# 22 filler matmuls at the head of TensorE's list, and the lists of the first two units arranged anew

## The chip, the core and the metric

The kernel runs on one core of a Trainium2 chip. Five engines work from lists of their own: TensorE (PE: matmuls and transposes; its weight loads are shown apart as PEld), VectorE (DVE), ScalarE (ACT), GpSimd (POOL) and SyncE (SP, which here only issues transfers). They wait for one another by semaphores. Transfers between HBM and SBUF run on 16 DMA engines that serve several queues: q1 is fed by SP, q0 by GpSimd, q10 by ScalarE. TensorE writes into eight PSUM banks, from which VectorE and ScalarE read. The metric is the device time of one execution, in microseconds, as a median over runs.

## The reference

For 4 batches, 8 heads, 768 positions and a head size of 64, each query keeps the 6 chunks (of 32 keys) with the highest bound, attends causally to them, and the result goes through a two-layer MLP.

```python
k_min = np.min(k_chunks, axis=3)
k_max = np.max(k_chunks, axis=3)
ub = np.sum(np.maximum(q * k_min, q * k_max), axis=-1)      # per query and chunk, shapes cut
top_chunks = np.argsort(np.where(causal, ub, -1e9), axis=-1)[..., -6:]
scores = np.where(sel & causal_in_positions, (q @ k.T) / 8, -1e9)
x = softmax(scores) @ v                                      # -> [3072, 512]
h = x @ w_in                                                 # [3072, 2048]
g = np.where(h > 0, h, np.exp(np.minimum(h, 0)) - 1)
out = g @ w_out                                              # [3072, 512]
```

## The kernel before

The 3072 rows are done in eight units of 384. Units 0 and 1 hold the first and second 192 positions of batches 0 and 1 together (in the names `p` and `s`, after the batch); units 2 to 7 are the halves of one batch each, from the second half of batch 0 on. In unit 0 no chunk has to be chosen, since at most 6 exist. For each unit the kernel loads q, k and v, transposes q and k on TensorE, takes each chunk's minimum and maximum of k on VectorE, computes the bounds, chooses, scores, takes the exponential on ScalarE, multiplies with v, divides, transposes, and runs the MLP.

**An order written out by hand.** The code first records a graph of operations with `g.op`, each with the engines that it may run on. Then it walks through a string, `ORDER`: every three characters are an engine's letter (P, A, D, G, S for TensorE, ScalarE, VectorE, GpSimd, SP) and the number of an operation. A second string, `PLACES`, gives each new buffer its slot. So the strings fix on which engine an operation runs, each engine's list, and which buffer follows which in a slot. An engine works strictly along its list: an operation that waits holds up all behind it. What reads or reuses a buffer waits for the operations before it on that buffer.

**The names used below.**

- `ldk`, `ldq`, `ldv` (L304): the loads of k, q and v, into tiles `f`. Eleven such tiles exist, and a load waits until the tile's earlier readers are done. Of units 0 and 1, `ldk1s00` is k of batch 1, unit 1, its first 96 positions.
- `kT`, `qT` (L402, four matmuls each): fp32 transposes of k and q with `ident_f`. One for each batch, unit and group of four heads. `kmax`, `kmin`, `ks` (L367, L370) are the chunks' extremes; `kt`, `qh`, `qt` (L320 on ScalarE, L322 on VectorE) copy the transposes out of PSUM; `ka` copies k into the tile `lhs`.
- `tr` (L684): one 512-column bf16 matmul that puts the mask into a bank ahead of unit 0's scores `sc` (L692). It needs `identb`, a bf16 copy of the identity that GpSimd makes in `ident` (L254), and `tn0`, `tn1` (L268). `ex` (L700) is the exponential.
- `v` (L333 on GpSimd, L322 elsewhere): the cast of loaded v. `pv` (L754): the product with v. `rcp`, `on` (L636, L646 on VectorE, L643 on ScalarE): the division. `px` and `xt` (L669): transposes of the result and their copies.
- `w_in0`, `w_in1`, `w_in2` (L291): loads of w_in, issued by GpSimd, columns for the groups fc 0 to 3, 4 to 7 and 8 to 15. `w_out0` to `w_out3` (L297) likewise.
- `h0.fc` (L851, four matmuls): the MLP's first layer for unit 0; `e`, `m`, `g` (L858, L860, L864) its activation; `o0.t.c` (L875) the second layer. `h0.4` to `h0.7` need w_in1, `h0.0` to `h0.3` w_in0, the others w_in2.
- `ub` (L592): the bound matmuls; `ubT`, `max`, `lt`, `sT` on VectorE (L603 to L620) choose the chunks; `mk` copies the choice into the tile that the scores of unit 1 (L728) read.
- Constants: `zeros`, `rz`, `sz`, `pz`, `pu`, `kz`, `ez`, `vz`, `kq` (memsets, L247), `es` (L276), `oh`, the one-hot pattern (L282, L285, 25 memsets), `tris` (L263), `ec` (L304, a transfer of the constant `econst` into `lhs`).

**Fillers.** The graph also holds 170 operations `fill`, each one matmul on the bf16 tile `zeros`. The string of before names none of them, so none runs:

```python
fills.append(g.op("fill", (PE,), lambda e, bank=bank: nc.tensor.matmul(
    ap(bank)[:, 0:256], lhsT=zeros[:, 0:P], rhs=zeros, start=True, stop=True),
    reads=[(fixed, "zeros")], writes=[(bank, 0)], after=fills[-2:-1]))
```

The walk through the strings:

```python
for j in range(0, len(order), 3):
    o = g.ops[64 * DIGITS.index(order[j + 1]) + DIGITS.index(order[j + 2])]
    for b in o.bufs:
        if b.slot is None and b.cls != "fixed":
            b.slot = DIGITS.index(next(places))
    o.emit({"P": PE, "A": ACT, "D": DVE, "G": POOL, "S": SP}[order[j]])
```

Of the kernel before, what the change touches and what calls it, by code (L numbers as in the profile page):

```python
# [39 lines left out]
G0iS0WD01A02D09D06S0sG0kD0jG0aS0yD03D00D0qG0mG0bA0VG04D05G0eS0uG0cG0dA0tS0rS0vS0xD0lD0oS0wS0YS0X  # L40
P0MD0OD0QS0BP1oP0DP1aP11S0ZS0zD0ED0NA0HA0IG0fG0gD0FP0KP1pA1eG0pP1kA0LD1bP0TA0RA15A17G16P1jP1tP1l
S0+D0UP1qP1uD1cP18A1nD13S2gS2fG0CA1rP1hD19A1sG0nP1zD12S2hS2iP1yA1iP1AA1gA1mGmED0PA1CP1vA1xA1BG0A
P1DP26P25P1ED10G0-S2PS2vS2OD27D28D1FA1wP1YP20P2aGmDA0SP29D2bP1XA2cP1+D21G0JP1IP1OP1RP1SP1HS2IP2o
P1ND1GD1JD1ZD1KP2dG1dGmFA1-P1LD2qD1PA1QD2jD22P23D1TD1UD2eA2sD24A1MS2QP1VD1WG08G2uG0hP2BD2DD2CA2t
Pm-Pn6G2EAn7GbsGmGPn2Gn8D2pG2rAm+Dn0D14D0GAn3Dn4P2wPmWA2xA2yS2RP2JA2KDn5D2zPmSPmODn9Dn1AmXAmTD2L
GmYPnaGmHDmZAmPP3lAnbGmIA2FDmQDmUPmKAmLDmVD3nD3mA2MD3pGncPnGG2HPniA2AG07GmMA1fPnCG2SAnjD3oPnuD3q
D3rPnmDmRDmNG3tPneAnHA3sGnkDndAnvGnIP3HDnlAnDPnqGnwA3IDnJP41PnyDnxAnrA3uGnEDnFP3JP3+AnfPnQDnsS2k
A3KDntD2NAnnS3fG3LP2XA42P38PnRS2mA40GmJAnzA2GDnoD2ZDnpD2YP4lGngPnKPnXA4mD3vDnhA2+A30D43D3cP4DA4E
P4FG3ePnYA4GGnAD3aA3dD39D2-D31P4jD4HP3gG3bP33PnSS32S4+A34D35PnLA3hA4kD3iG3kS2TDnBP3wD4nS2VG2lG36
D3xG3jS50PnZPn-A2nD3yD3zA37S4-D3APnMPnTD3BD3CS4YD3GA3EG3FP3NDnUP4OP4MS4XS4ZP3MD3DP48P45A4PA4NP44  # L50
G2UG2WP4aD3ODn+D3PP4IP4JA4bP3SPnNA49D46D47A3TD4cS7UP3QD4QAnOP4sP4uP4dA3RP4eP4oS7SA4tP4pD4fP5rG3U
D4gA4vP4RD4KD4LP4SP4hA5sP5QS7WD4TD4UP3VP3WA5RD4qP5fP4VD3XD3YA5gS7RP5ED4rG4wP4xA4WP4yD5SP3ZA5FD4z
P58D4AA5iS57P5kD5aA4iP4BA4CG7VS53P5JD3-P5xD59G5TG5uA5cS55D5BA5oA5NPolPoJD5mA5GD5KPo5S5wAoKD5zS8l
PoxD5yGoLAo6SaND5LA5IPo9A5tDoMSo0G5bPodGo7AomD5lS51AoyG5MPohDo8G5nAoaSnPGonPoRA5OScZGobDooAoePoF
D7TA5hGofAoSPopDocG5AA5jGozDogPo1AoGGoTSnVDoAAoqPoBGoHDoUS7NAoiGorA5DPotDoIS7OAo2GojDosP5VAouGo3
DokA5HGovDo4A5UG5PDowA5vPoNAoCG5dD5XPp1A52G7XD5WAoOD5ZGoDPp2A5qGoPA5eD5YPpePpfD5-SnWPp7D5+SaHPp8
DoEA60G61DoQPpgD63A56DaOP66P6gA67P64DaQP6cP6iA65Pp3D62A6dDaPA6jP6mP68A6hP6lD5pP6aDaRP6eA6nPp9A69
D54SaSG6oA6fP6BP6xD6kPoVA6bS7MA6CP6vA6yS7YP6qA6wP6HS7PP6pAoWP6zA6IS7QPoZD6rGoXD6sA6AG5CP6JDoYAo-
P6tScRP6MGbmP6ND6uA6KP7bGo+P7cP76A6OP6-Dp0PphA77D6LA7dD6PShFScXG7eDaTP6FA6+Pp4ApiA6GP6DA6EP72P70
P78P6RDp5A71A79DaUP6QDaVA73P7CP74A75P6YA6ZP7xP7zA7yA7ADaWP7ZD7aD6SSb3P6WA6XPpaApbP7DSpjSp6G7BP8g  # L60
A8hD7-D81D6TD7+P7rP7lP7fP7gP7tP89P7pD8iA7EG7FD7hD7iD8aD8bG8kG8jP7vP8yD8zA7mA7sA7qA7uP7nA7oA7wP8m
P6UP8FP7GScSSaCDb4A8CD8DG8EA6VA8dG8fP7HD7ID7JA8qP7jA7kP84A85P8tA8uAaIA8vD8oP7KD7LPpkPpEPpQPpsPpM
# [36 lines left out]
DwlDwdGwgDwhPvWPwyGwsAvXDvQDvRGvYDvZPwGAwHPv-Av+DwtPw2GwIDwJAw3Dw4Dw5AwzDwAGw0Dw1PwKPwmPwQAwnGwo
DwpPwCAwDDwBPwRPwLPwSGwEDwFPwTAwUPwWPwXSwVPwMPwNDwOSwPPwYPwZAw-Sw+Px0Px1Px2Px3Dx4Sx5  # L100
"""
PLACES = """
012034567000812349a10562170103125110304017213233236458001721210034522131062120134456670324031011
2206007710050120112732140001224010263151400156000721281724932a00b64251ac1657102d30416e1437016309
# [876 lines left out]
```

## Time and profile before

| | us |
|---|---|
| median of 3 runs (280.84 to 281.32) | 281.3 |
| profiled execution | 281.25 |
| its span, first to last instruction | 279.5 |
| TensorE busy | 263.2 |
| VectorE busy | 217.4 |
| ScalarE busy | 217.1 |
| GpSimd busy | 125.5 |
| moved by the DMA engines | 38.47 MB |

How to read the rows of the profile. A row of a timeline has the start (us from the first instruction), the duration, the engine, the line of the code, the operation, what it writes and reads, the shapes, how many instructions are merged, and in brackets the idle time before with what ended it. A row of the chain of waits has the start, the length and what the chain went through: it is followed back from the last instruction, at each step to what released it. A row by window has its bounds and length, then busy time and number of instructions of TensorE, its weight loads, VectorE, ScalarE and GpSimd, and then TensorE's granted clock, the mean busy share of the DMA engines (it can pass 1 where packets overlap) and GB/s. A row of a queue has the packets, the MB and their share of the DMA engines' time. A row of a transfer's issue has the median time from issue to landing as its last number.

### The profile page before, as it was taken

The numbers are of one execution on the slowest core, as the hardware profiler recorded it, in microseconds if no ns is written. First come the engines' busy times: TensorE is split into PE (matmuls) and PEld (weight loads), VectorE is DVE, ScalarE is ACT, GpSimd is POOL, SyncE is SP. The second block draws the span as 40 slices with busy tenths as digits, with TensorE's granted clock in tenths as the row PEclk, the third lists the DMA queues.
The fourth block names the chain that finished last, engine by engine and source line by source line (L and its number), as shares of the span: only waits on it lengthen the run. The fifth ranks groups of instructions, "written<-read, shape, count | busy, mean of one in ns | idle before, by whom it ended". The sixth has DMA issues, their size and how long they took to land.

```text
span 279.5 us, 6918 instructions
## 1 busy us (share of the span) xinstructions
PE 263.2 (94%) x2436; PEld 162.9 (58%) x2436; DVE 217.4 (78%) x656; ACT 217.1 (78%) x493; POOL 125.5 (45%) x249
## 2 busy tenths in 40 slices
PE   1978899999999999999999999999999999999994
PEld 0745465785456755576555555666655556665553
DVE  4668978799978999979998999569797698424931
ACT  2596796789699998999999859886968579982620
POOL 8674745348521755422685736222541346310410
PEclk9999999999999999999999999999999999999999
DMA  8999999999529999946985499416600210042002
GB/s 163 198 211 211 199 211 210 217 202 251 123 60 203 247 219 230 196 115 112 171 203 114 109 226 206 84 36 136 170 4 0 60 39 1 16 139 82 15 17 96
DMA packets 103779, 38.47 MB, mean 138 GB/s; under 512 B 95168, under 2 KB 99520, under 8 KB 103744
## 3 DMA queue, kind: packets, MB, share of 16 engines
q1 hardware_dynamic: 98864, 33.53, 57.3%
q0 software_dynamic: 3696, 4.19, 8.7%
q10 hardware_dynamic: 1184, 0.30, 0.5%
q8 instruction: 19, 0.31, 0.5%
q14 instruction: 16, 0.13, 0.1%
HBM read 30.41 MB, written 6.29 MB: 131 GB/s over the span
## 4 chain that ended last, share of the span: by engine, by line
PE 70%; DVE 13%; DMA 8%; ACT 4%; issue 1%; POOL 1%; SPq 0%; DVEq 0%; ACTq 0%
PE bank L875 24%; PE bank L851 22%; PE bank L782 9%; DMA w_in_sb<-in_moe_w_in_dram 5%; PE bank L833 5%; DVE gT L864 2%; PE bank L592 2%; PE bank L402 2%; DMA kc<-in_k_dram 2%; ACT e L858 2%; DMA f<-in_k_dram 1%; PE bank L543 1%; PE bank L728 1%; PE bank L893 1%; DVE on L646 1%
## 5 line engine op out<-in xcount | busy, mean ns | idle before, releaser
L851 PE MATMUL bank<-xt,w_in_sb 128*128 128x384 bf16 x512 | 89.2, 326 | 2.2 <-DMA w_in_sb<-in_moe_w_in_dram 2.2
L875 PE MATMUL bank<-w_out_sb,gT 128*128 128x512 bf16 x368 | 89.5, 379 | 0.0
L860 POOL TENSOR_SCALAR m<-e 128x384 f32<-128x384 f32 x96 | 50.7, 536 | 59.3 <-ACT e L858 47.0
L864 DVE SCALAR_TENSOR_TENSOR gT<-bank,m 128x384 bf16<-128x384 f32 x128 | 65.9, 549 | 9.7 <-POOL m L860 8.4
L858 ACT ACTIVATE e<-bank 128x384 f32<-128x384 f32 x128 | 58.6, 493 | 16.7 <-PE bank L851 13.9
L851 PEld LDWEIGHTS <-w_in_sb 128*128 128x128 bf16 x512 | 49.1, 98 | 36.6 <-DMA w_in_sb<-in_moe_w_in_dram 3.0
L797 ACT ACTIVATE pt<-bank 128x384 bf16<-128x384 f32 (+1 forms) x144 | 67.0, 547 | 3.5 <-PE bank L782 2.1
L875 PEld LDWEIGHTS <-gT 128*128 128x128 bf16 x368 | 34.6, 97 | 35.7 <-issue 2.2
L782 PE MATMUL bank<-rhs,lhs 96*128 96x384 bf16 (+2 forms) x240 | 42.8, 293 | 1.0 <-DVE on L646 0.5
L814 POOL TENSOR_TENSOR pt<-pt,tri 128x256 bf16<-128x256 bf16 (+1 forms) x18 | 16.6, 924 | 39.3 <-ACT pt L801 20.1
L782 PEld LDWEIGHTS <-lhs 96*128 96x128 bf16 x240 | 21.7, 97 | 13.9 <-issue 0.9
L833 PEld LDWEIGHTS <-pt 128*128 128x128 bf16 x576 | 21.0, 97 | 4.0 <-DVE pt L814 0.4
L833 PE MATMUL bank<-vext,pt 128*128 128x65 bf16 x576 | 22.2, 193 | 0.3 <-DVE pt L814 0.3
L646 DVE TENSOR_TENSOR on<-bank,rcp 128x384 bf16<-128x384 f32 (+1 forms) x37 | 18.8, 509 | 1.2
L367 DVE TENSOR_REDUCE kst<-bank 128x12 f32<-128x384 f32 x32 | 16.6, 548 | 3.7 <-PE bank L402 2.8
L322 POOL CAST rhs<-qt 64x384 bf16<-64x384 f32 x23 | 12.3, 542 | 13.1 <-ACT qt L320 12.1
L636 DVE RECIPROCAL rcp<-bank 128x6 f32<-128x6 f32 (+1 forms) x40 | 7.3, 185 | 14.0 <-PE bank L833 8.7
L320 ACT ACTIVATE o<-bank 128x512 f32<-128x512 f32 (+1 forms) x13 | 7.5, 587 | 13.0 <-PE bank L875 10.1
L322 DVE COPY o<-bank 128x512 f32<-128x512 f32 (+1 forms) x12 | 7.9, 663 | 12.0 <-PE bank L875 10.0
L860 DVE TENSOR_SCALAR m<-e 128x384 f32<-128x384 f32 x32 | 13.1, 417 | 2.8 <-ACT e L858 2.6
L402 PE MATMUL bank<-ident_f,f 96*128 96x96 f32 x64 | 9.3, 295 | 6.2 <-DMA f<-in_k_dram 6.2
L814 DVE TENSOR_TENSOR pt<-pt,tri 128x512 bf16<-128x512 bf16 (+1 forms) x30 | 10.8, 376 | 5.3 <-ACT pt L801 3.5
(102 smaller groups left out, 338.6 us busy)
## 6 DMA issues: line engine op xcount, KB each, us to landing
f<-in_v_dram SPq DMA_DIRECT2D x22, 256.0 KB, 4.8
out_dram<-o SPq DMA_DIRECT2D x21, 256.0 KB, 3.4
f<-in_q_dram SPq DMA_DIRECT2D x18, 256.0 KB, 4.9
f<-in_k_dram SPq DMA_DIRECT2D x18, 256.0 KB, 4.7
kc<-in_k_dram SPq DMA_DIRECT2D x8, 384.0 KB, 4.3
w_out_sb<-in_moe_w_out_dram POOLq DMA_DIRECT2D x4, 512.0 KB, 10.5
f<-in_q_dram SPq DMA_DIRECT2D x6, 192.0 KB, 5.0
w_in_sb<-in_moe_w_in_dram POOLq DMA_DIRECT2D x2, 512.0 KB, 8.8
```

Of the source, the lines that this page charges most:

```text
L322: eng[e].tensor_copy(out=dst, in_=src)
L367: g.op(("kmin", "kmax")[w] + tag, (DVE,), lambda e, w=w, op=op: nc.vector.tensor_reduce(out=cs(w), in_=src(), axis=AX.X, op=op), reads=[(b ...
L646: nc.vector.tensor_tensor(out=ap(on)[:, 0:nt].rearrange("p q h d -> p h q d"), in0=view()[:, :, :, 0:D], in1=ap(rcp)[:, :, 0:nt].to_broadc ...
L782: nc.tensor.matmul(ap(banks[hd])[:, o + pc:o + pc + wd], lhsT=apl(ls, G)[0:96, pr, hd, P * kb:P * (kb + 1)], rhs=ap(rs)[0:96, hd, c0 - HS ...
L797: lambda e, hd=hd, pt=pt, banks=banks, wtot=wtot: nc.scalar.activation(out=ap(pt)[:, hd, PAD:PAD + wtot], in_=ap(banks[hd])[:, 0:wtot], fu ...
L814: eng[e].tensor_tensor(out=view, in0=view, in1=tri[:, 64:64 + P].rearrange("p (a b w) -> p a b w", a=1, b=1) .to_broadcast([P, 2, len(dg), ...
L833: nc.tensor.matmul(view()[:, hd, qi, :], lhsT=ap(pt)[:, hd, P * qi + off:P * qi + off + P], rhs=ap(vx[b])[:, kb, 2 * r + hd, :], start=(kb ...
L851: nc.tensor.matmul(ap(bank)[:, 0:HS], lhsT=w_in_sb[:, kk, P * fc:P * (fc + 1)], rhs=ap(xT[i, kk]), start=(kk == 0), stop=(kk == NKK - 1))
L858: g.op(f"e{i}.{fc}", (ACT,), lambda e, eb=eb, bank=bank: nc.scalar.activation(out=ap(eb), in_=ap(bank)[:, 0:HS], func=AF.Exp), reads=[(ban ...
L860: g.op(f"m{i}.{fc}", (POOL, DVE), lambda e, eb=eb, mb=mb: eng[e].tensor_scalar(out=ap(mb), in0=ap(eb), scalar1=-1.0, scalar2=1.0, op0=AOT. ...
L864: nc.vector.scalar_tensor_tensor(out=ap(gt), in0=ap(bank)[:, 0:HS], scalar=0.0, in1=ap(mb), op0=AOT.max, op1=AOT.min),
L875: nc.tensor.matmul(ap(bank), lhsT=ap(gts[fc])[:, P * tt:P * (tt + 1)], rhs=w_out_sb[:, fc, :], start=(fc == 0), stop=(fc == NFC - 1))
```

## The change

Three things change; no computation does.

In the graph, all fillers share one bank:

```diff
     fills = []
+    bank = Buf("bank")
     for i in range(FILL):
-        bank = Buf("bank")
         fills.append(g.op("fill", (PE,), lambda e, bank=bank: nc.tensor.matmul(
```

`ORDER` and `PLACES` are new strings. `ORDER` names 1970 operations in place of 1948: the same ones, and 22 fillers. Their last 1313 operations are the same in both, on the same engines; the slots that the strings give differ all through. The first lines of the diff:

```diff
-G0iS0WD01A02D09D06S0sG0kD0jG0aS0yD03D00D0qG0mG0bA0VG04D05G0eS0uG0cG0dA0tS0rS0vS0xD0lD0oS0wS0YS0X
-P0MD0OD0QS0BP1oP0DP1aP11S0ZS0zD0ED0NA0HA0IG0fG0gD0FP0KP1pA1eG0pP1kA0LD1bP0TA0RA15A17G16P1jP1tP1l
...
+G0iS0WD00D01PjZA02D09Pj-S0sPj+D06G0cG0aG0mG0kD0lD0qPk0Pk1G0bS0yPk2Pk3D03D0jG04D0eG0fD05G0oG0nG08
+G0gS0uPk4A0VPk5A0tS0rPk6Pk7Pk8Pk9PkaP1kPkbPkcP1oPkdPkePkfP0MPkgP11P1aA15A1ePkhPkiP1tS0xA0QG0RG0d
...
```

Spelled out by the names of the operations, the heads of the lists:

```
TensorE before: kT0p1 tr kT0p0 kT1p1 kT1p0 qT0p0 tr tr qT0p1 tr tr sc0p0 sc0p1 tr qT1p0 qT1p1 tr tr sc1p1 sc1p0
                pv (15) kT0s0 pv pxp3 pxp0 pxp2 pxp1 kT0s1 h0.4 h0.6 h0.5
                qT0s0 h0.3 qT0s1 h0.2 h0.1 h0.7 ub00 h0.0 h0.15 h0.9 ...
TensorE after:  fill x14 tr fill x2 tr fill x3 kT0p1 fill kT1p0 kT1p1 fill x2 tr kT0p0 qT0p0 qT0p1 tr tr sc0p0 tr
                qT1p1 sc0p1 qT1p0 tr sc1p1 tr sc1p0 pv (of batch 0: 8, then of batch 1: 8) pxp3 kT0s0 pxp0 pxp2
                pxp1 kT0s1 h0.4 h0.6 h0.5 qT0s0 qT0s1 h0.3 h0.1 h0.2 ub00 h0.7 h0.0 h0.9 h0.15 ...
GpSimd before:  kz vo tn0 pu tn1 ident ez1 ez0 es0 es1 oh vz0 ka01p0 v0p1 rz w_in1 v0p0 v1p0 w_in0 ka10p0 ks1p1
                w_in2 tris2 ka10s0 kq ks0s1 ky202 w_out0 m0.6 ks0s0 m0.3 w_out1 w_out2 ...
GpSimd after:   kz ez0 tn0 pu vo tn1 ident es1 sz rz tris2 oh ka00p1 es0 v0p1 w_in1 ka11p0 v0p0 ka01p0 v1p0 w_in0
                w_in2 ka11p1 ks1p1 ka10p0 vc0 ks1p0 ky202 ka10s0 kq w_out0 m0.6 qa00s0 w_out1 m0.3 w_out2 ...
ScalarE before: table ldk1p00 ldk0p10 kt0p0 ka00p0 kt1p1 qh0p0 ka00p1 kt1p0 ka11p0 ex ex ex qh1p1 ka11p1 ex x5 ka10p1
ScalarE after:  table ldk1p00 ldk0p10 kt1p0 kt1p1 kt0p1 kt0p0 qh0p0 ka00p0 ex ex qh1p1 ex x4 ka10p1 ex ex
VectorE before: warm tnz triz kp idz zeros vz1 identb pz sz kmax0p1 kt0p1 kmin0p0 kmin0p1 kmax0p0 kmin1p1 qh0p1 ...
VectorE after:  zeros warm tnz triz pz vz1 idz kp ez1 identb vz0 kmax0p1 kmin1p1 kmax1p1 kmin0p1 kmin0p0 kmax0p0 qh0p1 ...
SP before:      ldk1p10 ldk0p01 ldq0p11 ldk0p11 ldk0p00 ldq0p00 ldq0p10 ldq0p01 ldq1p10 ldq1p00 ldv0p1 ldv1p0 ldv0p0
                ldv1p1 ldk0s10 ldk0s00 ldq0s00 ldq0s10 ldk1s10 ec000 ldk1s00 ec001 ldq1s00 ldq1s10 ldv0s0 ...
SP after:       ldk1p10 ldk0p01 ldq0p11 ldk0p11 ldk0p00 ldq0p10 ldq0p00 ldq0p01 ldq1p00 ldq1p10 ldv0p1 ldv0p0 ldv1p1
                ldv1p0 ldk0s10 ldk0s00 ldq0s10 ldq0s00 ldk1s00 ec000 ldk1s10 ec001 ldq1s10 ldq1s00 ldv0s0 ...
```

29 operations of the first two units change their engine: `ez1` and `vz0` go from GpSimd to VectorE, `sz` the other way, and some copies (`ka`, `qa`, `mk`, `xt`), differences `ks`, three divisions `on` and the activation step `m0.13` move too.

More of the change, by code (lines that the diff above doesn't have):

```diff
@@ L45 @@
[L45 to L50, printed above, removed]
@@ new lines @@
+P1ED1FD0PP1YP1NP1OP1XP2aP29GmDS2IGmFG1gG1dA1wP1+P1IP1SP20G0JD2bD2cD21P1HD1ZA1GP1RG2jP2dS2RS2QG14
+D22D1JD1KD1TD1PP2oD2qA1-A2eP1LD1QD1UGbsA2sG2uP23P1VD1WA24A1MP2BD2CD2DG0hGmGPm-Am+Dn0Dn1D2EPn6An7
+Gn8Pn2An3P2wA2tA2xG2zP2JA2KA2yPmWPmOPmSDn4D2pDn5AmXGmHGmYD2rAmPA2FAmTD2LD0GP3lDmQDn9A2APnaAnbGmI
+DmZDmUPmKGncD3nD3mD3pD3oDmVG2HG07PniPnGA2MAmLGmMD3qD3rAnHA1fS2kS32DmND2SDmRA3sAnjPnuAnvPnCPneDnd
+S3fGnIDnJP3HA3IAnDA3tGnkDnlPnmPnqAnrGnwDnxS2mGnEG3uDnFDnsDntP3JPnyP3+P41AnfGngPnQD2NP2XDnhG2GA3K
+G3LA3vAnzAnnDnoPnRGmJP4lA40A42A4mD2YP4FPnKP4DA2+A4GA30D2ZDnAA4EG4HPnXP38P4jPnYDnpD3aD3cD2-A4kA3d
@@ new lines @@
+P3gP33A34D3eD39D31D3bD43S2VS2TA3hA35G3kPnLPnSD3iP3wDnBD4nPnZPnMPn-PnTD3xD3yS50S4+A3jA2nS4-G37G36
+G2lP3ND3zD3AD3BD3CG2UD3GP4MP3MA3ES4ZS4YDnUG2WG3FD3DS4XP4JA4NP4OA4PD3OD3PP44P48A49Dn+P4aP45D46A4b
+D4cP4IP3SA3TPnND47D4QP3QP4uP4sP4dP4eD4fA3RAnOG3UP4oP4pP4SP4RP5rD4gP4hA4vA4tG4wD4qD4TD4KD4LA5sP5Q
+A5RD4UP3WP3VD3XD3YD5SP5fA5gP4VA4WD4rP5EA5iA5FP4xP4yS7US7SS7RP3ZP5kP58A4iD4zD4AP4BP5JD3-D5mD5aA5c
+A4CG7VS55S5wSaNS57D59P5xD5lA5oG5TPoJA5GD5KPo5AoKD5zPoxPolD5yGoLG5uAo6D5LA5IPo9G5bGo7A5tDoMPodG5M
+AomA5NSo0S7WD5BAoyPohDo8S8lG5nAoaGonPoRA5OSnPS51S53GobDooAoePoFScZD7TA5hGofAoSPopDocG5AA5jGozDog
@@ new lines @@
+Po1AoGGoTDoAAoqPoBGoHSnVDoUAoiGorA5DPotS7NDoIAo2GojDosP5VS7OAouGo3DokA5HGovDo4A5UG5PDowA5vPoNAoC
+G5dD5XPp1A52G7XD5WAoOD5ZGoDPp2A5qGoPA5eD5YPpePpfD5-Pp7D5+SnWPp8DoESaHA60G61DoQPpgD63A56DaOP66P6g
+A67P64DaQP6cP6iA65Pp3A6dD62A6jDaPP6mP68A6hP6lP6aD5pP6eA6nDaRPp9A69G6oA6fP6BD54P6xSaSPoVA6bD6kA6C
+S7MP6vA6yP6qA6wS7YP6HP6pAoWS7PP6zA6IPoZD6rGoXD6sA6AS7QG5CP6JDoYAo-P6tP6MGbmP6ND6uA6KP7bGo+ScRP7c
+P76A6OP6-Dp0PphA77D6LA7dD6PP6FDaTPp4A6+G7eApiShFScXA6GP6DA6EP72P70P78P6RDp5A71A79DaUP6QDaVA73P7C
+P74A75P6YA6ZP7xP7zA7yA7ADaWP7ZD7aD6SSb3P6WA6XPpaApbP7DSpjSp6G7BP8gA8hD7-D81D6TD7+P7rP7lP7fP7gP7t
@@ L101 @@
+DjTPjBPvuPvEDjwDjxSjyAjIGjPAjAAjGAjEPjUAjCPjVDjWDjXSjYPvFPvvPvGPvHDvIDvwPw6Aw7SvxPvKAvLGvMDvNSvJ
+PwiPwuAwjAwvDwkPwqAwrDwwDw8Dw9PvSAvTGvUDwxPwaAwbDwcPweAwfPvOAvPDvVDwlDwdGwgDwhPvWPwyGwsAvXDvQDvR
+GvYDvZPwGAwHPv-Av+DwtPw2GwIDwJAw3Dw4Dw5AwzDwAGw0Dw1PwKPwmPwQAwnGwoDwpPwCAwDDwBPwRPwLPwSGwEDwFPwT
+AwUPwWPwXSwVPwMPwNDwOSwPPwYPwZAw-Sw+Px0Px1Px2Px3Dx4Sx5
 """
 PLACES = """
[L103 to L104 removed]
@@ L118 @@
+52600432124970010200f210001732143257083412564315422141355143620000216211622301202011040011311522
+6101022d341097031425201c00212a74612b010121326504203ef1702g61130412674052057360715647011101253570
+60132003270141475230155647203011120023200182510041210101b7226002dg1133500241c1122272601e102f6030
+1541729112071
 """
```

115 lines of the change are left out of this document (49 added, 66 removed).

## The prediction

> **What bounds the kernel now.** I read the page first, for the engine that is full and the stretch where it is not, then busy time by stretch, then the chain of waits up to 80 us, then the timelines of TensorE and GpSimd, and last the transfers.
>
> ```profile
> PE 263.2 (94%) x2436; PEld 162.9 (58%) x2436; DVE 217.4 (78%) x656; ACT 217.1 (78%) x493; POOL 125.5 (45%) x249
> PE   1978899999999999999999999999999999999994
> DMA  8999999999529999946985499416600210042002
> 0.00:6.00 6.00, 0.39 (x1) 0.18 (x1) 2.85 (x11) 1.49 (x2) 5.15 (x16) 1.00 0.83 155
> 6.00:13.00 7.00, 6.44 (x40) 4.90 (x42) 4.34 (x9) 3.09 (x7) 4.05 (x28) 1.00 1.35 203
> 21.50:31.50 10.00, 7.93 (x80) 4.74 (x80) 8.66 (x29) 6.86 (x17) 6.48 (x13) 1.00 1.17 206
> 31.80:80.00 48.20, 48.20 (x449) 30.00 (x450) 42.75 (x138) 39.05 (x86) 24.23 (x48) 1.00 0.95 189
> ```
>
> In the window rows the first pair after the length is TensorE. From 31.8 to 80 us it has no gap (48.20 of 48.20), so what reaches it earlier there reaches the end earlier, until another engine or a transfer runs out of lead. Before that it has gaps: 5.61 us of the first 6, and 2.07 of the 10 us up to 31.5. The transfer engines are full in the same stretch: their digit is 9 from the second slice on, 200 GB/s.
>
> ```profile
> 2.36 4.15 DMA f<-in_k_dram
> 17.33 0.50 POOL lhs L322
> 17.91 0.16 POOL kst L370
> 18.06 13.64 DMA w_in_sb<-in_moe_w_in_dram
> 31.75 4.07 PE bank L851 x24
> 25.89 0.82 PE L851 MATMUL bank<-xt,w_in_sb 128*128 128x384 bf16 x4 [1.04 <-DMA w_in_sb<-in_moe_w_in_dram]
> 31.75 4.07 PE L851 MATMUL bank<-xt,w_in_sb 128*128 128x384 bf16 x24 [1.19 <-DMA w_in_sb<-in_moe_w_in_dram]
> ```
>
> Five rows of the chain, two of TensorE's timeline. The chain goes from the third w_in load, issued by GpSimd at 18.06 and landed at 31.70, straight to TensorE's first matmul on it at 31.75. GpSimd issued it late: two small operations of its list stood before it. So the end is set by when w_in2 lands, not by how fast TensorE does its first 30 us.
>
> **The 22 fillers.** Each is a 256-column matmul on zeros. The rate is that of the early bf16 matmuls on the mask constant:
>
> ```profile
> 7.73 2.56 PE bank L402 x16
> 10.29 0.85 PE bank L684 x2
> 44.12 0.66 PE bank L402 x8
> 44.78 1.73 PE bank L875 x8
> 2.15 0.17 DVE L247 MEMSET zeros<- 128x128 uint32 x1
> 6.56 0.74 PE L402 MATMUL bank<-ident_f,f 96*128 96x96 f32 x3 [0.76 <-DMA f<-in_k_dram]
> ```
>
> Early, 512 columns take 0.85/2 = 0.425 us; late, 1.73/8 = 0.216. Transposes: 0.160 against 0.082. TensorE runs at half rate at first, though the granted-clock column says 1.00 throughout. A filler at the early rate costs 0.21 us. `zeros`, now first on VectorE, is ready near 1.1 us. Fourteen fillers end at 1.1 + 14 x 0.21 = 4.1. A mask matmul then needs ident_b, whose cast moves to about 4.0 to 4.5 with one more memset ahead of ident on GpSimd (an estimate); it, two fillers, a second mask matmul and three fillers bring TensorE to 4.5 + 2 x 0.425 + 5 x 0.21 = 6.4. The first key transposes can't finish before their second load, at 6.51. Nineteen fillers cost nothing under that wait; if identity or zeros came 0.5 us later they would push the transposes by 0.4. The three behind cost 0.3 to 0.6 us of TensorE's list, with 2 to 3 us of lead behind them, as follows.
>
> **What faster early matmuls are worth.** Between 6.56 and 12.63 TensorE does 6.07 us of work at half rate. If the fillers end that state by 6.5, up to 3.0 us are saved. Taken to the end, that would give 281.25 - 3.0 = 278.2. I value it at zero, since the next users are held elsewhere: unit 0's attention waits for v, which GpSimd casts, and MLP 0 for w_in. [...]
>
> **The arranged lists: GpSimd issues w_in earlier.** This is the term that I count.
>
> ```profile
> 5.99 3.10 POOL L285 MEMSET onehot<- 32x1 bf16 x24
> 11.66 0.50 POOL L322 COPY lhs<-kt 64x384 bf16<-64x384 bf16 x1 [1.98 <-ACT kt L320]
> 12.13 0.61 POOL L333 TENSOR_SCALAR vext<-f 64x512 bf16<-64x512 f32 x1
> 12.80 1.37 POOL L247 MEMSET rhs<- 32x1536 bf16 x1
> 14.12 0.98 POOL L291 DMA_DIRECT2D w_in_sb<-in_moe_w_in_dram  x1
> 15.18 1.35 POOL L333 TENSOR_SCALAR vext<-f 128x512 bf16<-128x512 f32 x2
> 16.48 0.80 POOL L291 DMA_DIRECT2D w_in_sb<-in_moe_w_in_dram  x1
> 4.48 1.12 POOL L276 TENSOR_SCALAR_AFFINE_SELECT econst<-econst 32x384 bf16<-32x384 bf16 x2
> f<-in_v_dram SPq DMA_DIRECT2D x1, 128.0 KB, 4.6
> f<-in_v_dram SPq DMA_DIRECT2D x1, 128.0 KB, 5.2
> ```
>
> Now: one-hot done at 9.1, 2 us idle for a key copy of ScalarE, v, the 1.37 us memset `rz`, w_in1 at 14.12. After: `rz` (1.37), `sz` (about 0.3) and `tris2` (about 0.25) stand ahead of the one-hot, `ez1` (half of 0.85) goes to VectorE and `es0` (0.56) behind it: 9.1 + 1.37 + 0.3 + 0.25 - 0.43 - 0.56 = 10.0. The key copy now waits for an earlier one on ScalarE and takes 0.5, es0 0.56: 11.1. Then v, whose load lands at 6.75 + 4.6 = 11.4 as before: cast to 12.1, and w_in1 issues at 12.1, 2.0 us earlier. After it 0.98, two key copies (0.5 each) and a cast (0.65) make 14.7; the next cast waits for the load issued at 9.42 that lands at 14.6: 15.4. w_in0 issues at 15.4 (1.0 earlier), w_in2, next to it, at 16.3 (1.8 earlier).
>
> What that brings at landing has two ends. The stream of three loads starts 2.0 us earlier and the transfers are full, so at best w_in2 lands 2.0 earlier, at 29.7. If the pause between w_in1 and w_in0 stays tied to w_in0's issue, it is 1.0, at 30.7. I take 1.5, between them, since w_in2's own issue moves by 1.8 but has to queue behind w_in0. TensorE's other work must be done by then. w_in1 lands about 2 us earlier, at 20.4 or so; from there eight groups h0.x (4 matmuls, 4.07/6 = 0.68 us each), 0.7 of query transposes and 0.8 of bound matmuls make 6.9, so 27.3. From w_in0's landing (25.89 less 1.0, so 24.9) five groups and the bounds make 4.2, so 29.1. It is done either way.
>
> **What is given back.** The transfers were full already, so an earlier w_in pushes the q and k loads on SP's queue.
>
> ```profile
> q0 software_dynamic: 1163, 1.68, 92.5%
> q1 hardware_dynamic: 1158, 0.35, 23.6%
> q0 software_dynamic: 471, 0.48, 96.3%
> q1 hardware_dynamic: 395, 0.10, 23.0%
> f<-in_q_dram SPq DMA_DIRECT2D x1, 192.0 KB, 23.4
> f<-in_q_dram SPq DMA_DIRECT2D x1, 192.0 KB, 5.1
> 43.95 0.82 PE L402 MATMUL bank<-ident_f,f 96*128 96x96 f32 x8
> ```
>
> The first pair is 22 to 32 us, the second 17 to 20: packets go one for one, and since those of q0 are larger, q1 falls to 0.035 MB/us. [...] In rows: the last q load of batch 1 for unit 1 is issued at 18.63 and lands 23.4 later, at 42.0; its transposes run at 43.95, so 1.95 us of lead. A gain of 1.5 uses most of it. I take off 0.1 for the places where lead runs out.
>
> Sum: 281.25 (profiled execution, span 279.5 and 1.75 around it; the median of the three is 281.3) - 1.5 + 0.1 = 279.85, that is 279.9.
>
> **The rivals.**
>
> *The early half rate was the bound*: 278.2, as worked out. For it: TensorE is full from 6 to 13. Against: the 1.04 and 1.19 us waits for w_in. Chance 0.06.
>
> *The gain is eaten by the transfers.* By 42 us as many bytes have to be moved as before. If w_out3, the next load of GpSimd, also comes 1.5 to 2 us earlier, it gets between: 512 packets beside q1's last loads, at 116 packets/us 4.4 us for both, of which half is q1's own. The q load then lands near 42.0 + 2 = 44.0, and its transposes stand where they stood, at 43.95. TensorE waits there instead of at 31.75: 281.2. Against: w_out3 hangs on GpSimd's order behind several MLP operations, and a pause of q0 just before it lets q1 catch up. Chance 0.20.
>
> *The first q loads of unit 1 starve*, the slower side. Now the second is issued at 13.24, lands at 18.3 and is through before w_in's packets come (from about 16.9, 2.8 us behind the issue). After, w_in's packets come from 14.9, when about 2 us x 0.2 MB/us = 0.42 MB of q1, 1,700 packets, is still to go ahead of it. Some 400 pass beside w_in1 in 3 us. If q0 makes no pause before w_in0, the other 1,300 go at 116 per us: 11.2 us, so it lands at 14.9 + 3.1 + 11.2 = 29.2. TensorE stands at these transposes, with 0.7 + 3 x 0.65 + 0.8 + 2 x 0.65 = 4.7 us to do before w_in2's groups: 29.2 + 4.7 = 33.9 against 31.75, 2.2 slower, 283.4. With a pause such as that of now at 20 us,
>
> ```profile
> q0 software_dynamic: 21, 0.02, 14.1%
> q1 hardware_dynamic: 1072, 0.33, 94.3%
> q0 software_dynamic: 71, 0.06, 25.0%
> ```
>
> it lands before 24 and costs nothing: the first row is 16 to 17 us, w_in's first packets, the others are 20 to 21.5, where q1 moved 0.33 MB. It decides from a landing at 31.75 - 4.7 = 27.0 on. Half a pause gives the case's middle: 282.3. Chance 0.24.
>
> **How the numbers follow.** Forecast 0.50 at 279.9, its own range 279.1 to 280.6; early clock 0.06; eaten 0.20; starved 0.24. Low end 278.8: w_in2 at 2.0 earlier and 0.4 of the clock's gain kept. High end 282.6: into the starved case beyond its middle. About 0.2 % (0.56 us) is what a measurement can tell. Faster: 0.50 + 0.06 + 0.02 of the eaten case = 0.58; same: 0.17 of it; slower: 0.24 + 0.01.
>
> **What would show it.** Right: w_in's three issues on GpSimd near 12.1, 15.4 and 16.3; the first matmuls on w_in2 near 30.2; TensorE full from there; fillers done by 6.5; early transposes at 0.08 us instead of 0.16. Wrong: the chain leads through f<-in_q_dram to L402 between 22 and 30 (starved), or TensorE has a gap near 42 (eaten); h0.x follow each other without a wait for w_in (early clock was the bound).

## The result, and the profile after

The changed kernel takes 284.28 us (median of four runs, 283.19 to 285.15) where the kernel before took 281.07 beside it (four runs, 280.42 to 281.32): ratio 1.0104, 95% interval 1.0082 to 1.0127. It is slower by 1.0%, some 2.9 us. The profiled execution took 285.15 us with a span of 283.4, so 3.9 us more span than the profiled one of before. Lines of the code stand one further down than in the rows of before, those near the bank of the fillers apart; the experiments without fillers are numbered as before. One run of the experiments (287.07 us, with `rz` late, 2.7% above the fastest of its kernel) was slow and counts in no ratio.

The timeline of TensorE, of the kernel after, answers to the rows of before at 6.56, 25.89 and 31.75:

```profile
1.14 3.17 PE L932 MATMUL bank<-zeros 128*128 128x256 bf16 x14 [1.14 <-DVE warm L248]
5.79 0.39 PE L685 MATMUL bank<-trineg,ident_b 128*128 128x512 bf16 x1 [1.49 <-DVE ident_b L260]
6.45 0.49 PE L932 MATMUL bank<-zeros 128*128 128x256 bf16 x3
7.22 0.82 PE L403 MATMUL bank<-ident_f,f 96*128 96x96 f32 x8
7.88 0.38 PE L932 MATMUL bank<-zeros 128*128 128x256 bf16 x2
8.32 0.82 PE L403 MATMUL bank<-ident_f,f 96*128 96x96 f32 x8
26.83 2.12 PE L852 MATMUL bank<-xt,w_in_sb 128*128 128x384 bf16 x12 [1.98 <-DMA w_in_sb<-in_moe_w_in_dram]
32.56 3.42 PE L852 MATMUL bank<-xt,w_in_sb 128*128 128x384 bf16 x20 [1.39 <-DMA w_in_sb<-in_moe_w_in_dram]
41.56 0.60 PE L729 MATMUL bank<-rhs,lhs 96*128 96x128 bf16 x6 [0.67 <-DVE gT L865]
61.31 0.49 PE L852 MATMUL bank<-xt,w_in_sb 128*128 128x384 bf16 x2
62.53 1.79 PE L852 MATMUL bank<-xt,w_in_sb 128*128 128x384 bf16 x10 [0.73 <-ACT xt L321]
```

With the fillers TensorE is at full rate early: eight key transposes start at 7.22 and the next matmul at 7.88, which is 0.08 us each, against 0.16 before. But both waits for w_in are longer (1.98 and 1.39 against 1.04 and 1.19), the first matmul on w_in2 stands at 32.56, 0.81 later than in before, and TensorE has two waits, 0.67 and 0.73 us, in a stretch where it had none.

A further wait grows later, where the lists of both kernels are the same. The timelines of TensorE and VectorE, of the kernel after:

```profile
100.53 0.34 PE L670 MATMUL bank<-ident_b,on 128*128 128x128 bf16 x3 [1.68 <-DVE on L647]
98.75 0.84 DVE L485 TENSOR_TENSOR kn<-kc 96x512 f32<-96x512 f32 x1 [1.55 <-DMA kc<-in_k_dram]
```

Before, the first stood at 97.04 with a wait of 0.55. VectorE waits for a load of k (`kc`) that landed 6.1 us after its issue here and 4.9 in before. This makes 1.1 of the 3.9 us of the two profiled runs, and it is not steady: with the fillers taken out of the changed kernel, the load took 4.9 us and TensorE waited 0.63. The profiled run is the slowest of its four.

Why w_in is late stands on GpSimd and VectorE. The timelines of the two, of the kernel after:

```profile
3.03 0.53 POOL L248 MEMSET vext<- 128x96 bf16 x1
3.72 0.49 DVE L248 MEMSET vext<- 64x520 bf16 x1 [1.55 <-POOL vext L248]
4.29 0.17 DVE L248 MEMSET ident_f<- 128x128 f32 x1
4.52 0.29 POOL L255 TENSOR_SCALAR_AFFINE_SELECT ident_f<-ident_f 128x128 f32<-128x128 f32 x1 [0.64 <-DVE ident_f L248]
5.61 0.59 POOL L277 TENSOR_SCALAR_AFFINE_SELECT econst<-econst 32x384 bf16<-32x384 bf16 x1 [0.79 <-DVE econst L248]
8.67 3.15 POOL L286 MEMSET onehot<- 32x1 bf16 x24
13.66 0.99 POOL L292 DMA_DIRECT2D w_in_sb<-in_moe_w_in_dram  x1
17.07 1.56 POOL L292 DMA_DIRECT2D w_in_sb<-in_moe_w_in_dram  x2
```

GpSimd's memset of vext (`vo`) now stands behind the 0.95 us one of pt. VectorE's other memset of vext (`vz1`) has to come after it (the code names `vo` as what `vz1` needs), and waits 1.55 us. Behind `vz1` stand VectorE's memsets of ident_f and of econst, for which GpSimd waits in its turn, 0.64 and 0.79 us. The one-hot ends at 8.67 + 3.15 = 11.82, and w_in is issued at 13.66, 17.07 and about 17.9. Only the second of these, w_in0, is later than in before (16.48). That was enough: in all fourteen profiled kernels w_in2 landed 5.7 to 5.9 us behind w_in0, though it was issued from 0.8 to 1.6 us behind it. The chain of waits of the kernel after goes the same way; six of its rows:

```profile
3.09 0.47 POOL vext L248
3.72 0.49 DVE vext L248
5.10 0.39 DVE econst L248
17.07 9.71 DMA w_in_sb<-in_moe_w_in_dram
26.83 1.49 PE bank L852 x8
39.36 1.56 DVE rhs L323
```

From w_in0's landing at 26.78 the chain goes on through TensorE's first matmuls on it, the activation on ScalarE and VectorE and a cast of VectorE, to TensorE's wait at 41.56. The landing of w_in2 at 32.5 is no longer on it.

The q loads give no wait. The transfers' issues in the kernel after have, for the load of SP at 13.27 and the two at 17.89 and 18.61:

```profile
f<-in_q_dram SPq DMA_DIRECT2D x1, 192.0 KB, 4.9
f<-in_q_dram SPq DMA_DIRECT2D x1, 192.0 KB, 13.8
f<-in_q_dram SPq DMA_DIRECT2D x1, 192.0 KB, 18.3
```

They land at 18.2, 31.7 and 36.9; the last was at 42.0 before.

### The profile page after: what moved, and what is told of

Same layout as the page of the kernel before. It is cut to its first block, busy times and chain, and to the rows that moved or that the text cites. A ratio compares the mean times of both kernels' runs of the same rounds, so it can differ in the third digit from the quotient of the medians.

```text
span 283.4 us, 6965 instructions
## 1 busy us (share of the span) xinstructions
PE 264.7 (93%) x2458; PEld 163.3 (58%) x2458; DVE 218.1 (77%) x655; ACT 216.9 (77%) x490; POOL 126.9 (45%) x250
## 4 chain that ended last, share of the span: by engine, by line
PE 65%; DVE 14%; POOL 6%; ACT 6%; DMA 6%; issue 3%; POOLq 0%; ACTq 0%; DVEq 0%
PE bank L876 23%; PE bank L852 20%; PE bank L783 9%; PE bank L834 5%; DMA w_in_sb<-in_moe_w_in_dram 3%; ACT e L859 3%; DVE gT L865 2%; DMA kc<-in_k_dram 2%; PE bank L593 2%; PE bank L544 2%; DVE thr L612 1%; POOL m L861 1%; PE bank L894 1%; DVE kn L494 1%; ACT rhs L321 1%
## 5 line engine op out<-in xcount | busy, mean ns | idle before, releaser
L861 POOL TENSOR_SCALAR m<-e 128x384 f32<-128x384 f32 x95 | 50.1, 534 | 66.8 <-ACT e L859 54.1
L368 DVE TENSOR_REDUCE kst<-bank 128x12 f32<-128x384 f32 x32 | 16.3, 546 | 4.3 <-ACT kt L321 4.0
L321 ACT ACTIVATE kt<-bank 128x384 bf16<-128x384 f32 x13 | 6.2, 490 | 11.5 <-PE bank L403 5.4
```

Source lines behind the costliest of these rows:

```text
L321: nc.scalar.activation(out=dst, in_=src, func=AF.Copy)
L861: g.op(f"m{i}.{fc}", (POOL, DVE), lambda e, eb=eb, mb=mb: eng[e].tensor_scalar(out=ap(mb), in0=ap(eb), scalar1=-1.0, scalar2=1.0, op0=AOT. ...
```

## The experiments

Twelve kernels, each run in alternation with the kernel before on the same chip (not the same one for all), so the ratio is the measure; eleven are in the table, and the twelfth, made wrongly, is told below. "w_in2" is TensorE's first matmul on the third w_in load, "MLP 1" its first matmul of the second pass of the MLP, both from the one profiled run ("no wait": TensorE comes to it later than it lands). These two columns are rough: in eight of the profiled runs TensorE's mean granted clock was 0.987 to 0.994, by which some 3 to 7 us were at half (last section).

| kernel | median us | ratio to before, 95% | w_in2 | MLP 1 |
|---|---|---|---|---|
| before | 281.07 to 281.49 | 1 | 31.75 | 59.89 |
| after | 284.28 | 1.0104, 1.0082 to 1.0127 | 32.56 | 61.31 |
| after, no fillers | 284.61 | 1.0116, 1.0103 to 1.0129 | 32.42 | 61.17 |
| before, with fillers | 280.80 | 0.9978, 0.9964 to 0.9991 | 30.90 | 59.34 |
| after, `vz1` late | 283.42 | 1.0063, 1.0047 to 1.0079 | 30.90 | 59.82 |
| after, `xts2` first | 284.56 | 1.0105, 1.0084 to 1.0127 | no wait | 61.83 |
| first unit's lists only | 280.88 | 0.9991, 0.9979 to 1.0002 | 31.20 | 59.62 |
| before, with the wait | 281.38 | 1.0004, 0.9995 to 1.0013 | 31.41 | 59.64 |
| before, fillers, `rz` late | 280.91 | 0.9989, 0.9974 to 1.0005 | no wait | 58.45 |
| second unit's lists only | 282.74 | 1.0053, 1.0034 to 1.0072 | 31.77 | 60.46 |
| `vz1` late, third part old | 282.16 | 1.0035, 1.0018 to 1.0052 | no wait | 61.20 |
| `vz1` late, second part old | 282.09 | 1.0038, 1.0018 to 1.0058 | 31.07 | 59.62 |
| `vz1` late, cast late | 282.72 | 1.0053, 1.0035 to 1.0072 | 31.05 | 59.43 |

**The fillers taken out, and the fillers alone.**

```diff
-TensorE: fill x14 tr fill x2 tr fill x3 kT0p1 fill ...
+TensorE: tr tr kT0p1 ...                              (after, no fillers)
```

> The kernel after without its 22 fillers; everything else as after. My theory (the loss sits in GpSimd's and VectorE's new lists, the fillers only open the clock): the early transposes go back from 0.08 to 0.16 us each, but the time stays within 0.6 us of after, 283.7 to 284.9, since first exps hang on VectorE's and ScalarE's readers of the same banks; w_in issues stay at 13.7, 17.1, 17.9. Rival (the fillers themselves cost, by power or by holding the first transposes back): about the time of before, 281 to 282. Second rival (the early clock carries part of the new lists): slower, 285.5 to 287.

```diff
-TensorE: kT0p1 tr kT0p0 ...        VectorE: warm tnz triz kp idz zeros ...
+TensorE: fill x22 kT0p1 tr ...     VectorE: zeros warm tnz triz kp idz ...   (before, with fillers)
```

> The lists of before, with only the zeros (first on VectorE) and the 22 fillers at the head of TensorE's list added. My theory: the fillers are harmless and early transposes run at 0.08 instead of 0.16 us; w_in2 still lands near 31.7 and holds its matmuls, so the time is that of before within 0.6 us, 280.3 to 281.3. Rival (fillers cost): 282.5 or more. Rival of the prediction (the early half rate was the bound): 278.2, three us faster.

Without the fillers the changed lists took 1.16% more than before instead of 1.04%: the intervals overlap, so there they bring nothing that can be told. On the lists of before they bring 0.22%, 0.6 us, and this is the one kernel whose whole interval lies below 1. So no part of the loss is seen to come from the fillers. By the profile, their gain comes through GpSimd: the groups by line on GpSimd up to 19 us have the key copies, before and then before with fillers, with the idle time ahead of them last:

```profile
L322 POOL COPY lhs<-kt 64x384 bf16<-64x384 bf16 x2 | 1.0, 494 | 2.0 <-ACT kt L320 2.0
```

```profile
L323 POOL COPY lhs<-kt 64x384 bf16<-64x384 bf16 x2 | 1.0, 496 | 1.7 <-ACT kt L321 1.6
```

Earlier transposes make ScalarE's key copy earlier, GpSimd's idle time is 0.3 us shorter, and w_in goes out at 13.82, 16.04 and 17.63 against 14.12, 16.48 and 18.06. w_in2's first matmul stands 0.85 earlier. It follows w_in0, which landed 0.82 earlier (25.02 against 25.84) for an issue 0.44 earlier; why twice as much, is left open.

**The wait for vext taken away, and put into the kernel before.**

```diff
-VectorE: zeros warm tnz triz pz vz1 idz kp ez1 identb vz0
+VectorE: zeros warm tnz triz pz idz kp ez1 identb vz1 vz0     (after, vz1 late)
```

> The kernel after with one move: VectorE's second memset of vext, which waits for GpSimd's, stands behind the cast of ident_b instead of ahead of it. My theory (this wait is what delayed GpSimd's one-hot and w_in): the one-hot ends 0.8 to 1.2 us earlier than 11.8, w_in1 issues near 12.6 and w_in0 near 16, w_in2 lands 1 us earlier than 32.5, time 0.8 to 1.3 us below after, about 283.2. Rival (w_in0 is held by a v load's landing or by a key copy of ScalarE, not by this wait): w_in1 earlier, w_in0 and w_in2 as in after within 0.3, time within 0.4 of after.

```diff
-GpSimd:  kz vo tn0 pu tn1 ident       VectorE: warm tnz triz kp idz zeros vz1 identb
+GpSimd:  kz tn0 pu vo tn1 ident       VectorE: warm tnz triz vz1 kp idz zeros identb   (before, with the wait)
```

> The kernel before with the wait alone: GpSimd's memset of vext behind that of pt, VectorE's ahead of that of ident_f (so that VectorE waits 1 us for GpSimd, and GpSimd then for ident_f). My theory (the wait costs only where GpSimd's list has no idle time behind it; in before the 2.0 us in front of its first key copy swallow it): the one-hot ends about 1 us later, w_in is issued as in before within 0.3, time 281.1 to 281.9. Rival (the wait costs wherever it is put, since the transposes wait for ident_f too): w_in 0.8 later and 282.1 or more.

With `vz1` late, GpSimd's timeline is what the prediction's sum for it had forecast (12.1, 15.4 and 16.3):

```profile
7.31 3.15 POOL L286 MEMSET onehot<- 32x1 bf16 x24
12.30 0.99 POOL L292 DMA_DIRECT2D w_in_sb<-in_moe_w_in_dram  x1
15.53 1.56 POOL L292 DMA_DIRECT2D w_in_sb<-in_moe_w_in_dram  x2
```

w_in2's matmul is at 30.90 instead of 32.56 (w_in2 landed at 30.86; the profile puts the end of the wait down to VectorE's `ubT`, 0.03 us later, so w_in2 was not alone in holding it). The loss falls from 1.04 to 0.63%: the wait is worth 0.4% (1.2 us; the intervals of the two ratios leave 0.03 to 0.8%). The same wait in the kernel before costs nothing that can be measured (1.0004): there GpSimd idles 2 us ahead of its first key copy, and the wait only shortens that. The change spent this idle time on three operations put ahead of the one-hot (`sz`, `rz`, `tris2`), so the wait went through to w_in.

**The copy `xts2` ahead of `kt010`.**

```diff
-ScalarE: ... xts3 qa0010 qt012 xts1 kt010 xts2 kt011
+ScalarE: ... xts3 qa0010 qt012 xts1 xts2 kt010 kt011      (after, xts2 first)
```

> The kernel after with one move on ScalarE: the copy xt (group 2 of the second MLP's input) ahead of the key copy that waits for VectorE's key maxima, as in the lists of before. My theory (this order made the 0.9 us that after loses around 62.5 us): the matmuls at 62.5 start 0.6 to 0.9 us earlier and the time is 0.5 to 0.9 below after, 283.4 to 283.8. Rival (the next wait, for the maxima themselves, takes its place): within 0.3 of after.

1.0105: no gain, the rival was right. The wait of 0.73 for xt went, and two others came in its place, 0.34 us at 66.23 for VectorE's gT and 0.22 at 67.26 for a key copy of ScalarE. So one copy is not the cause. That VectorE's and ScalarE's lists of this stretch are late together is how the two new waits read; no run shows it.

**The two units apart.** The lists of one part were taken from the change and of the rest from before; a few of the slots had to be given anew.

```diff
+preamble, first unit: lists of after, vz1 late, fillers;  second unit on: lists of before   (first unit's lists only)
+preamble, first unit: lists of before, no fillers;        second unit on: lists of after    (second unit's lists only)
```

> The change's lists for the first unit and the preamble (with the fillers, and with VectorE's memset of vext behind the cast of ident_b as in the run with that move alone), and the lists of before for everything from the second unit on. My theory (of the 2.8 us that the change loses, some 1.6 come from the second unit's lists, at 41 and at 62 us, and what is behind; the first unit's lists lose only by the wait for vext): w_in2 lands near 30.9, the matmuls at 60 us stand 0.3 to 0.8 earlier than in before, no 0.7 us waits at 41 and 62.5, time 280.2 to 281.1. Rival (the second unit's waits come from what the first unit's lists leave late): the gaps at 41 and 62 stay, 282.5 to 283.5.

> The mirror: the lists of before for the preamble and the first unit, without fillers, and the change's lists from the second unit on. My theory: w_in is issued and lands as in before (w_in2 near 31.7), then a wait of 0.6 near 41 and one of 0.7 near 62 appear, time 1.2 to 2.5 over before, 282.7 to 284.0. Rival: 281.1 to 281.9, and what the change lost came with the first unit.

> The mirror made anew: the lists of before for the preamble and the first unit, no fillers, the change's lists from the second unit on (in the first mirror VectorE's reciprocals stood up to eight places further ahead through the whole kernel, so its time says nothing of this). My theory (the second unit's lists lose about 2 us by themselves, since the run with them stood 0.63% over before and the run without them 0.09% under): w_in2 lands near 31.7, waits near 41 and 62, 0.6 to 0.9% over before, 282.9 to 283.7. Rival (they lose only beside the first unit's new lists): within 0.3% of before.

The first mirror was made wrongly: VectorE's reciprocals stood up to eight places too far ahead all through. It took 289.45 us (1.0295, 1.0273 to 1.0316), and tells only what such a shift costs. In its timeline VectorE stands in front of a reciprocal whose operand isn't there, with other work behind it.

```profile
122.14 0.20 DVE L636 RECIPROCAL rcp<-bank 128x6 f32<-128x6 f32 x1 [1.79 <-PE bank L833]
```

Made anew, the second unit's lists alone cost 0.53% (0.34 to 0.72). From the other side: all lists of the change but the wait stand 0.63% over before, the first unit's alone 0.09% under, so the second unit's make 0.72%. That is 1.5 to 2.0 us, the larger part of the loss. The first unit's lists without the wait brought no gain that can be told (0.9991, 0.9979 to 1.0002), though w_in went out as early as forecast. In the second unit's lists alone w_in2's matmul is where it was (31.77 against 31.75), and the two waits come all the same, in TensorE's timeline:

```profile
40.71 0.60 PE L728 MATMUL bank<-rhs,lhs 96*128 96x128 bf16 x6 [0.61 <-DVE gT L864]
61.68 2.60 PE L851 MATMUL bank<-xt,w_in_sb 128*128 128x384 bf16 x15 [0.73 <-ACT xt L320]
```

**The second unit cut in two.** Both start from the kernel with `vz1` late.

```diff
+lists of before from the transposes qT011 on (about 52 us)          (third part old)
+lists of before for the second unit up to that point, after behind  (second part old)
```

> The run with VectorE's memset moved alone (0.63% over before), with the lists of before from the transposes of the third batch of q on (about 52 us), the second unit's lists before that point as in the change. My theory: the wait of 0.7 to 0.8 us at 62 goes, the one near 40 stays, 0.9 to 1.3 us under that run: 0.15 to 0.35% over before, 281.6 to 282.2. Rival (the wait at 62 only moves): 0.5 to 0.7% over, 282.6 to 283.2.

> The other half: the same run with the lists of before for the second unit up to that point, and the change's from there on. My theory: the cast of VectorE near 38 takes 0.35 instead of 1.56 us, the wait of 0.67 near 40 goes, the one at 62 stays, 0.5 to 0.8 us under that run: 0.3 to 0.5% over before, 282.0 to 282.6. Rival (the two halves cost only together): as before, within 0.1%.

0.35 and 0.38%, against 0.63 with both parts new: each part is worth 0.25 to 0.3%. Each of these is a difference of two ratios with a margin of some 0.25, so it is likely that both count, and how they share the loss is not shown. The waits go each with its own part: the third part old has none at 62, the second part old none at 40. In the profiled run of the third part old, TensorE is late for another reason (its clock, in the last section); the ratio is that of twelve runs.

**The cast of VectorE.**

```diff
-VectorE: ... m0.11 g0.11 qa10s1 g0.8 m0.10
+VectorE: ... m0.11 g0.11 g0.8 qa10s1 m0.10      (cast late)
```

> The run with VectorE's memset moved alone, with one more move: VectorE's cast of rhs from qt (1.56 us while GpSimd copies lhs and multiplies pt by tri) behind the product gT that TensorE waited for. My theory (the cast is stretched by what GpSimd does beside it, and TensorE's wait of 0.67 near 40 is that stretch): the wait goes or is under 0.3, time 0.3 to 0.7 us under that run: 0.4 to 0.5% over before, 282.3 to 282.7. Rival (VectorE's whole list is late there): the wait stays and the time is within 0.1% of that run, 282.7 to 283.2.

What stood in front of the wait at 40 is in the timelines of VectorE and GpSimd with `vz1` late:

```profile
37.70 1.56 DVE L323 CAST rhs<-qt 64x384 bf16<-64x384 f32 x1
39.29 0.56 DVE L865 SCALAR_TENSOR_TENSOR gT<-bank,m 128x384 bf16<-128x384 f32 x1
37.67 0.50 POOL L323 COPY lhs<-kt 64x384 bf16<-64x384 bf16 x1
38.14 0.91 POOL L741 TENSOR_TENSOR pt<-pt,tri 128x384 bf16<-128x384 bf16 x1
```

and with the cast late, VectorE, GpSimd, TensorE:

```profile
37.25 1.20 DVE L865 SCALAR_TENSOR_TENSOR gT<-bank,m 128x384 bf16<-128x384 f32 x2
38.49 0.92 DVE L323 CAST rhs<-qt 64x384 bf16<-64x384 f32 x1
38.27 0.91 POOL L741 TENSOR_TENSOR pt<-pt,tri 128x384 bf16<-128x384 bf16 x1
39.55 0.60 PE L729 MATMUL bank<-rhs,lhs 96*128 96x128 bf16 x6 [0.18 <-DVE rhs L323]
```

Before, the same cast took 0.35 us. In both rows here it ends 0.2 us behind GpSimd's product. The wait of TensorE falls from 0.67 to 0.18, and MLP 1 starts 0.4 earlier (59.43 against 59.82). The time is 0.53% over before, at the edge of the rival's range and not apart from 0.63. So the cast does make this wait, and what the wait costs at the end is too small to be told.

**GpSimd's memset of rhs behind w_in.**

```diff
-GpSimd: ... v0p1 rz w_in1 v0p0 v1p0 w_in0 ka10p0 ks1p1 w_in2 tris2
+GpSimd: ... v0p1 w_in1 v0p0 v1p0 w_in0 ka10p0 ks1p1 w_in2 rz tris2    (before, fillers, rz late)
```

> The lists of before with the 22 fillers, and GpSimd's 1.37 us memset of rhs behind the issue of w_in2 instead of ahead of w_in1. By the prediction's term 3 (an earlier issue brings an earlier landing): w_in1 at 12.5, w_in0 near 15, w_in2 near 16.5, 1.1 earlier than in the run with fillers on the lists of before; w_in2 lands 0.5 to 1 us earlier than 30.86, time 280.0 to 280.4. Rival (the three loads are bound by what shares the transfers, not by their issue): w_in1 lands earlier, w_in2 within 0.3 of 30.86, time 280.5 to 281.1.

w_in is issued at 12.23, 14.53 and 16.12, and w_in2 lands at 29.12, 1.7 earlier than with fillers alone. MLP 1 starts 1.4 us earlier than in before. Yet the time is 0.9989, not apart from before nor from the fillers alone. TensorE's timeline shows what came and went:

```profile
24.80 0.47 PE L403 MATMUL bank<-ident_f,f 96*128 96x96 f32 x3 [1.77 <-DMA f<-in_q_dram]
37.48 0.85 PE L403 MATMUL bank<-ident_f,f 96*128 96x96 f32 x8 [0.74 <-DMA f<-in_k_dram]
96.26 0.34 PE L670 MATMUL bank<-ident_b,on 128*128 128x128 bf16 x3 [1.21 <-DVE on L647]
224.28 4.55 PE L852 MATMUL bank<-xt,w_in_sb 128*128 128x384 bf16 x27 [0.64 <-DMA xt<-on]
```

The first is the prediction's starved q load: issued at 12.83, it landed 11.9 us later (5.0 or 5.1 in before). At the second TensorE waits for a k load, where it had no wait in before; TensorE came to w_in2 2.1 us earlier than in before, and 0.7 of that is gone by MLP 1. The third row stood at 97.04 in before with a wait of 0.55: of the 1.44 us at MLP 1, 0.78 are left. There the gain goes with the kc load and what follows it on VectorE, here in before and then with `rz` late:

```profile
95.12 0.69 DVE L484 TENSOR_TENSOR kn<-kc 96x512 f32<-96x512 f32 x1 [0.28 <-DMA kc<-in_k_dram]
```

```profile
94.09 0.95 DVE L485 TENSOR_TENSOR kn<-kc 96x512 f32<-96x512 f32 x1 [0.69 <-DMA kc<-in_k_dram]
93.99 0.51 POOL L323 COPY lhs<-kt 64x384 bf16<-64x384 bf16 x1 [0.91 <-ACT kt L321]
```

VectorE waits longer for the load, GpSimd's key copy starts 0.1 us ahead of the product, and the product takes 0.26 longer. At 224 TensorE waits 0.64 for a transfer, where it has no wait in before. Whether every early run pays this way is left open: it is one profile, and the other runs reach from 279.50 to 281.87, the one of 287.07 apart.

## Why the prediction was wrong, by its own steps

The forecast was 279.9 and no case of it held 284.3.

- **Term 3, GpSimd issues w_in earlier: this step failed first.** It let GpSimd's new list run freely, and asked only for the v loads and ScalarE's keys. The change had moved `vo` behind `pu`, and the sum didn't ask who waits for `vo`. With that one wait gone the issues are 12.30, 15.53 and 16.34, within 0.2 us of the sum; with it they are 13.66, 17.07 and 17.9. The term was to bring 1.5 us; TensorE's first matmul on w_in0 came 0.94 later (26.83 against 25.89), that on w_in2 0.81 later.
- **Its size was wrong as well.** Issues 1.8, 0.95 and 1.7 earlier than in before brought w_in2's matmul 0.85 earlier (30.90), not 1.5. The bound at 1.0, from a pause tied to w_in0's issue, was the better one, since w_in2 landed 5.7 to 5.9 us behind w_in0 in every profiled kernel. And the time gained nothing that can be told even so (0.9991 with the first unit's lists alone).
- **What the sum left out: the second unit's lists.** "From 31.8 to 80 us it has no gap ... so what reaches it earlier there reaches the end earlier" was read off the lists of before, and used for lists in which 29 operations had changed engines. It got no term, and cost 1.5 to 2.0 us, with waits of TensorE both before and behind 52 us. A stretch that is full with one order is not full with another.
- **Term 1, fillers at no cost: right.** The nineteenth ends at 6.9 (6.45 + 0.49) instead of 6.4, since ident_b came behind `vz1` too: the first mask matmul stands at 5.79, not 4.5.
- **Term 2, the early clock at zero: right for the changed lists as far as can be told, too low for those of before,** where it brought 0.6 us. That the fillers end the half rate was supposed, and the run with them alone shows it: sixteen transposes took 1.48 us there (from 7.21) and 2.77 in before (from 7.52). What in the hardware ends it, no run shows. The prediction named v and w_in as the holders, but GpSimd's w_in itself stood behind a key copy that waits for ScalarE, whose input the transposes make. In the changed lists the time went elsewhere, as ScalarE's and VectorE's timelines of the kernel after show:

```profile
9.04 2.88 DVE L368 TENSOR_REDUCE kst<-bank 128x12 f32<-128x384 f32 x6 [2.65 <-ACT kt L321]
12.01 0.49 ACT L321 ACTIVATE kt<-bank 128x384 bf16<-128x384 f32 x1 [3.00 <-DVE kst L368]
13.35 1.08 ACT L701 ACTIVATE pt<-bank 128x512 bf16<-128x512 f32 x2
```

VectorE's first key reduction waits 2.65 us for a key copy of ScalarE, and ScalarE's next copy of a key bank then waits 3.00 us for VectorE's maximum and minimum of it, the last of six in a row. So the first exp is at 13.35, against 13.16 in before, though the keys' transposes, with the first of q, were done at 9.1 (8.32 + 0.82) instead of 10.3 (7.52 + 2.77). The graph gives no order between two reads of a buffer: `Graph.op` puts a read only behind writes. Here two readers of a bank did wait, once each way, 2.65 and 3.00 us; what made them, no run shows. So in these lists the order of a bank's readers was part of the schedule.

- **Term 4, 0.1 given back:** too small where it could be seen. In the kernel with `rz` late TensorE was 2.1 us ahead at w_in2 and 1.4 at MLP 1; 0.7 more went by 96 and 0.6 by 225.
- **The rivals.** The half rate was not the bound: the fillers alone brought 0.6 us, not 3.0. The q loads neither starved nor came late in the changed kernel. That w_in came late is not the whole reason: with `vz1` late w_in1 went out at 12.30, and the q load issued at 13.12 landed after 7.1 us, with no wait of TensorE. Starving showed in the kernel with `rz` late, at the place and of the kind that was forecast. There w_in0 followed w_in1 after 2.30 us instead of 3.23, which fits the prediction's condition of no pause between them; no run isolates it. It cost at most the 0.5 us by which TensorE came to w_in2 (29.6) after its landing (29.1). The eaten gain couldn't show in the changed kernel, which had none; the wait of 0.74 for a k load with `rz` late is of that kind, though not the load that was named. The slower side was right in sign, by another mechanism.

## What to carry to other kernels

An operation that is moved back on one engine delays not only its own engine: look up every operation on other engines that must follow it, and what stands behind those. Idle time ahead of a wait is what absorbs such a delay (here GpSimd's 1.98 us, at 1.0004); a change that fills it makes every later slip count. When lists change in a stretch that was full, that stretch needs its own walk through the new order; that it was full before says nothing.

## What was not expected of the hardware

**VectorE beside GpSimd.** A cast of 64x384 from SBUF took 0.35 us in before, with GpSimd idle, and 1.56 or 0.92 here beside GpSimd's copy and product, and ended 0.2 us behind them in both. So did the one in the run of the third part old: 1.56 us, ended at 40.35, the product at 40.13. What holds the cast until then, no run shows. VectorE's gT, which reads a bank, ran beside GpSimd's copy (37.81 to 38.31) in 1.20 for two; one took 0.56 in before at 37.72, with GpSimd idle.

**The clock falls back in one run and not in the next.** With `vz1` late and with the cast late, all instructions up to 37 us are the same. In the row by window from 14 to 16 us, first the one, then the other:

```profile
14.00:16.00 2.00, 2.00 (x15) 1.04 (x14) 0.21 (x1) 1.86 (x4) 2.00 (x4) 0.50 1.39 211
```

```profile
14.00:16.00 2.00, 2.00 (x36) 1.17 (x31) 1.21 (x3) 2.00 (x5) 1.97 (x4) 1.00 1.37 198
```

The granted clock was 0.50 in one and 1.00 in the other, with 15 and 36 matmuls in the same 2 us. With the rows around it (0.80 from 12 to 14, 0.85 from 16 to 18) the first stretch at half rate went from 13.2 to 16.6, some 3.4 us. In the run of the third part old there was one more, in the row

```profile
23.00:27.00 4.00, 4.00 (x18) 2.24 (x18) 1.96 (x5) 1.26 (x3) 1.54 (x3) 0.57 1.14 205
```

where TensorE has no gap (4.00 us busy of 4.00) and is itself the bound. Of the fourteen profiled runs eight have a mean granted clock of 0.987 to 0.994, the other six 0.997 to 1.000; at half, that makes some 3 to 7 us in each of the eight. Five of the eight have fillers. So the fillers bring the full rate early (1.48 us for sixteen transposes instead of 2.77) but do not keep it; what takes it back, and when, no run shows. The loss doesn't come from this: three of the four runs of the changed kernel had a mean granted clock of 1.000, and took 283.19 to 285.15 us.
